# Seven products for eight in the first unweighted group of a fused attention and routed-MoE kernel

## The chip, the cores and the metric

The kernel runs on one core of a Trainium2 chip, in fp32 throughout. The metric is the device time of one execution in microseconds, as a median of several executions. The engines are named as the profile names them: PE is TensorE (matmuls; PEld are its weight loads), DVE is VectorE, ACT is ScalarE, POOL is GpSimd and SP is SyncE, which only issues DMAs. PSUM is the memory that TensorE writes to, here used as eight banks of 128 partitions x 512 fp32.

## The reference

Two stages, joined by `x`. The first is a linear attention with a polynomial sketch as feature map; the second routes all rows over eight experts with balanced weights and adds up eight two-layer networks.

```python
# q, k, v: (4, 4, 1088, 32); S1, S2: (8, 32)
phi(x): a = S1 x;  b = S2 x;  features = all products a_i * b_j      # 64 features
kv  = sum over s of phi(k) v;  z = sum over s of phi(k)
x   = (phi(q) kv) / (phi(q) z + 1e-6)                                # -> x: (4352, 128)

P = exp(x @ w_gate - max)                                            # (4352, 8)
for _ in range(8):
    P /= P.sum(1) + 1e-9;  P /= P.sum(0) + 1e-9;  P *= N / E
out = sum over e of P[:, e] * (relu(x @ w1[e]) @ w2[e])              # w1: 128x1024, w2: 1024x128
```

## The kernel before

**One stream of steps.** TensorE's work of the second stage is cut into steps by a generator. The work of attention and of the routing is put between these steps: `fill(n)` takes steps from the generator until their shares add up to n, and every `yield n` of `attention(b)` or `routing()` is passed to `fill`. So the experts' matmuls fill the time in which attention waits for other engines. What can be computed before the routing weights exist is done without them (the unweighted groups) and kept in `kept`; weights are multiplied in later.

```python
# (first column, columns of a tile, tiles, experts, weighted)
groups = [(0, 256, 2, [0], False), (512, 288, 2, [0], False), (0, 256, 2, [1], False),
          *((1088 + 832 * i, 416, 2, [0], False) for i in range(3)), (3584, 384, 2, [0], False),
          (512, 384, 2, [1], False)]
DIRECT = (0,)
# ... five weighted groups of three tiles and a last one of two follow
```

An item is a group with one of its experts; an item of a two-tile group has four blocks of two rows of 128 hidden units by two tiles of columns. A block has four steps; each step is one first-layer product, made of two matmuls in the two halves of the array (64 output rows each), and a ReLU on ScalarE:

```python
def first(k, f, lo, hi, out, flip):
    ph = bank()[:, 0:hi - lo]
    for s in (1, 0) if flip else (0, 1):
        nc.tensor.matmul(ph[64 * s:64 * s + 64], w1[...], x[:, lo:hi], ..., tile_position=(0, 64 * s))   # L926
    nc.scalar.activation(out=out, in_=ph, func=Act.Relu)                                                 # L930
```

**The second layer of a block.** Its products follow eight steps (`LAG`) behind its first layer. A plain block is a 2x2 by 2x2 product of matrices with eight half products (`eight`). The others take the known scheme with seven (`seven`), which needs sums of weights `ws` (four GpSimd additions per expert, made once), and per block differences of hidden units on VectorE (one operation of two tiles, two of one tile):

```python
def eight(k):            # only groups in DIRECT; two PSUM banks
    return [[(w2[:, 2 * q + c // 2, 64 * s:64 * s + 64], h[c], c % 2, s, 0) for s in range(2)] for c in range(4)]

def seven(k):            # all other two-tile groups; four PSUM banks s0 .. s3
    ...                  # p1 .. p7, from w2, ws, h and the differences ts
    return bank0, [p2, p4], bank2, [p7]     # p7 is alone in its step

def sums(c):             # inside two(k): VectorE, L943
    if direct_of(j):
        return
    ...
    elif c == 4:
        less(t13, later_h, earlier_h)           # two tiles at once
    elif c == 5:
        less(ts[2], h[3], ts[0])
        less(ts[3], h[2], ts[2])

share = n / 480 * (16 / 15 if g in DIRECT else 1)     # what a step yields to fill
```

When the sums of a direct group are complete, two ScalarE copies put them into `kept`. For the others `part_of_seven` makes nine ScalarE copies and six VectorE additions.

**Attention of the first batch element** ends with quotients: numerators and denominators are made by TensorE (`fractions`) and divided on VectorE (`divide`), in three chunks of columns.

```python
def bank():              # next of the four rotating PSUM banks, tag "a"
    ...
def fractions(c, m):
    t = queries[0, c, "pn", m] = mps.tile([P, 512], F32, tag=f"s{m + 2}", name="s") if c else bank()
    for i in range(2):
        nc.tensor.matmul(t[64 * i:64 * (i + 1), 0:n], kvz..., phs[0]..., ...)        # L404

def divide(c):           # VectorE: transpose pd (L415), add 1e-6, reciprocal,
    ...                  # transpose back (L420), multiply pn into xT (L422)
```

The order in which it is entered, with steps between:

```python
        query_products(2, 0); keys_products(1, 0)      # L387; VectorE L336
        fill(0.75)
        query_products(2, 1)
        multiply(2, 0)                                  # VectorE L396, reads a bank of query_products
        keys_products(1, 1)
        fill(0.75)
        multiply(2, 1)
        fill(0.75)
        fractions(2, 1); fractions(2, 0)
        keys_products(1, 2)
        fill(0.75)
        divide(2)
        ...
        fill(0.5)
        for b in range(1, B):
            for n in attention(b):
                fill(n)
```

**Attention of the other batch elements:**

```python
    def attention(b):
        keys_sums(b)                    # TensorE L352, one bank()
        times(b, 0)                     # VectorE L465: in place, features of a times b
        yield 2.2 if b == 1 else 2
        keys_kept(b)
        times(b, 1)
        tops(b, 0)                      # TensorE L474, L478
        if b == 1:
            transpose_q(2)              # VectorE L302
        yield 1.4
        times(b, 2)
        over(b, 0)                      # VectorE L487, L489, L493
        tops(b, 1)
        ...
        over(b, 2)
        take_over(b, 0, W9, nc.gpsimd)  # DMAs from GpSimd's queue, L498, L500
        yield 0.7
        keys_ab(b + 1)                  # TensorE L319, L324
        yield 0.7
        if b == 1:
            transpose_q(3)              # VectorE L302
        keys_products(b + 1, 0)
        yield 1.4
        keys_products(b + 1, 1)
        if b == 1:
            queries_ab(3)               # TensorE L438
        ...
```

`times(1, ...)` needs `rb`, which a DMA brings (`repeat_b`).

Of the kernel before, what the change touches and what calls it, by code (L numbers as in the profile page):

```python
# [10 lines left out]
F32 = mybir.dt.float32  # L11
# [39 lines left out]
def kernel(  # L51
# [13 lines left out]
    P = nc.NUM_PARTITIONS  # L65
# [20 lines left out]
    mps = ctx.enter_context(tc.tile_pool(name="mps", bufs=1, space=PSUM))  # L86
# [7 lines left out]
    def bank():  # L94
        return aps.tile([P, 512], F32, tag="a", name="a")
# [56 lines left out]
    for i in range(2):  # L152
        t = wk.tile([P, H + 1, NT + 1, D], F32, name=f"v{i}", bufs=1)
# [144 lines left out]
    keys, queries = {}, {}  # L298
# [42 lines left out]
    def keys_sums(b):  # L341

        kp, vx = products.pop(b), v_slots[b % 2]
        pv = bank()[:, 0:128].rearrange("p (i c d) -> p i c d", i=2, c=2)

        slots = [slice(h, H + 1, H - h) for h in range(H)]

        for t in range(NT + 1):
            n = P if t < NT else 64
            for h in range(H):  # L350
                i, s = divmod(h, 2)
                nc.tensor.matmul(pv[64 * s:64 * (s + 1), i], kp[0:n, H * t + h].rearrange("p i j -> p (i j)"),  # L352
                                 vx[0:n, slots[h], t, :], start=(t == 0 and i == 0), stop=(t == NT and i == 1),
                                 tile_position=(0, 64 * s))
        sums_of[b] = pv
# [42 lines left out]
    def fractions(c, m):  # L398

        lo, hi = chunks[c]  # L400
        n = hi - lo
        t = queries[0, c, "pn", m] = mps.tile([P, 512], F32, tag=f"s{m + 2}", name="s") if c else bank()
        for i in range(2):
            nc.tensor.matmul(t[64 * i:64 * (i + 1), 0:n], kvz[:, m, i].rearrange("p h d -> p (h d)"),  # L404
                             phs[0][:, i, lo:hi], start=True, stop=True, tile_position=(0, 64 * i))
# [57 lines left out]
    def times(b, c):  # L463
        ph = third(phs[b % 2], c)
        nc.vector.tensor_tensor(ph, ph, third(rb, c), op=Alu.mult)  # L465
# [53 lines left out]
    def attention(b):  # L519


        follows = b + 1 < B
        keys_sums(b)
        times(b, 0)
        yield 2.2 if b == 1 else 2
        keys_kept(b)
        times(b, 1)
        tops(b, 0)
        if b == 1:
            transpose_q(2)  # L530
        yield 1.4
        times(b, 2)
        over(b, 0)
        tops(b, 1)
        if b == 1:
            queries_ab(2)
            repeat_a(2)
        if follows:
            repeat_b(b + 1)
        yield 1.4  # L540
        over(b, 1)
        if b + 1 == B:
            take_over(b, 0, 192, nc.gpsimd)
        yield 1.4
        tops(b, 2)
        if follows:
            transpose_k(b + 1)
        if b + 2 < B:
            load_k(b + 2)
            load_v(b + 2)  # L550
        yield 1.4
        over(b, 2)
        if b + 1 < B:
            take_over(b, 0, W9, nc.gpsimd)
        else:
            take_over(b, 192, W9, nc.sync)
        if follows:
            yield 0.7
            keys_ab(b + 1)
            yield 0.7  # L560
            if b == 1:
                transpose_q(3)
# [4 lines that stand above are left out]
                queries_ab(3)  # L567
                repeat_a(3)
            yield 1.4
            keys_products(b + 1, 2)  # L570
            yield 1.4
# [75 lines left out]
    PLAIN = len(groups)  # L647


    DIRECT = (0,)  # L650
    for lo in (1280, 512, 2048, 2816, 3584):
        groups.append((lo, NT3, 3, list(range(2 if lo == 512 else 1, E)), True))
    groups.append((0, 256, 2, list(range(2, E)), True))
# [3 lines left out]
    items = [(g, e) for g, group in enumerate(groups) for e in group[3]]  # L657
    loaded_w, sources, sums, parts, done = {}, {}, {}, {}, {}
    soon, later = [], []

    def direct_of(j):
        return items[j][0] in DIRECT

# [3 lines left out]
    def prepare_w(j):  # L667
        g, e = items[j]
        three = groups[g][2] == 3
        if j == 0:  # L670
            loaded_w[j] = first_w
        elif items[j - 1][1] == e or not groups[g][4]:
            before = [i for i in range(j) if items[i][1] == e and i in loaded_w]
            loaded_w[j] = loaded_w[before[-1]] if before else load_w(e, False)
            if three and tiles_of(j - 1) == 2:
                loaded_w[j] = *loaded_w[j][0:2], sums_of_four(e, loaded_w[j][1])
        else:
            loaded_w[j] = load_w(e, not three, again=groups[g][4])
            if three:
                if g == len(groups) - 2 and e in groups[-1][3]:  # L680
                    sums_of_two(e, loaded_w[j][1], True)
                loaded_w[j] = *loaded_w[j][0:2], sums_of_four(e, loaded_w[j][1])
# [46 lines left out]
    def part(g, k):  # L729

        if g in DIRECT:
            lo, n, _, es, _ = groups[g]
# [359 lines left out]
    def into(g, w, x, i, s, place):  # L1092

        lo, n, t, es, _ = groups[g]
        if g not in sums:
            banks = range(2 * g, 2 * g + 2) if g in DIRECT else range(4)
            sums[g] = [mps.tile([P, 512], F32, tag=f"s{i % 4}", name="s")[:, 0:n * (t - 1)] for i in banks]
# [6 lines left out]
        per = len(es) * (FO // (4 if t == 3 else 2)) * TIMES[t][i][s]  # L1104
        if g in DIRECT:
            per = FO
# [14 lines left out]
    def steps():  # L1121

        todo, sums_at, t = {}, {}, 0
        for k in range(len(blocks) + 5):
            if k == len(blocks) - 2:
                ctx.enter_context(tc.manual_schedule(engines={engines.DVE, engines.PE, engines.Activation}))
            if k == len(blocks):
                for i, ps in enumerate(last_products()):
                    todo.setdefault(t + i, []).extend(ps)
            if k < len(blocks):  # L1130
                j, q = blocks[k]
                g, e = items[j]
                lo, n, tiles, es, weighted = groups[g]
                if q == 0:
                    for i in (j, j + 1, j + 2 if 0 < j and j + 2 < first_weighted else j):
                        if i < len(items) and i not in sources and (pools or i < first_weighted):
                            prepare_x(i)
                        if i < len(items) and i not in loaded_w and (pools or i < first_weighted):
                            prepare_w(i)
                if j == 0 and q == 2:  # L1140
                    prepare_w(2)
                if q == 1 and j + 1 < first_weighted and not direct_of(j + 1) and loaded_w[j + 1][2] is None:
                    w1, w2, _ = loaded_w[j + 1]
                    w = w1, w2, sums_of_two(items[j + 1][1], w2)
                    loaded_w.update({i: w for i in loaded_w if items[i][1] == items[j + 1][1]})
                if q == 0:
                    if weighted and 1 <= es.index(e) <= es[0] + 1:
                        weigh_kept(g, es.index(e) - 1)
                if k == len(blocks) - HELD:
                    kept_to_sums(g)  # L1150
                m, step, sums_ = (four if tiles == 3 else two)(k)
                products = twenty if tiles == 3 else eight if g in DIRECT else seven
            for c in range(m if k < len(blocks) else 4):
                if k < len(blocks):
                    step(c)
                for do in sums_at.pop(t, ()):
                    do()
                while soon:
                    soon.pop(0)()
                for b, p in todo.pop(t, ()):  # L1160
                    second(b, p)
                if k < len(blocks) and c == 0:
                    for i in range(2, 10):
                        sums_at.setdefault(t + i, []).append(lambda i=i, f=sums_: f(i))
                    if k < len(blocks) - 2:
                        for i, ps in enumerate(products(k)):
                            todo.setdefault(t + LAG + i, []).extend((k, p) for p in ps)
                share = n / 480 * (16 / 15 if g in DIRECT else 1)
                if k >= len(blocks):
                    while later:  # L1170
                        later.pop(0)()
                elif later and (tiles == 3 or c % 2 or share > 0.9):
                    later.pop(0)()
                yield share
                t += 1
        while soon:
            soon.pop(0)()
        while later:
            later.pop(0)()
# [105 lines left out]
```

## Time and profile before

| quantity | before |
|---|---|
| time, median of 3 | 920.73 us (920.6 to 921.01) |
| span of the profiled execution | 919.0 us |
| PE matmul records (two for each fp32 matmul) | 7450 |
| idle time that PE spent waiting for named engines | 3.0 us in five waits |
| DVE, ACT, POOL busy | 75%, 46%, 23% |

How to read it: the profile is of one execution. Its page gives busy time by engine, the chain of work that ended last, and groups of instructions; L with a number is the line of the kernel before. Groups such as `a<-xT,w` name output and inputs: `a` is a rotating PSUM bank, `s` one of the banks of sums, `hb` hidden units, `kp` products of keys, `ph` products of queries. Records of TensorE overlap, since the two halves of its array work side by side, and the ends of matmuls are modelled.

### The profile page before, as it was taken

The numbers are of one execution on the slowest core, as the hardware profiler recorded it, in microseconds if no ns is written. First come the engines' busy times: TensorE is split into PE (matmuls) and PEld (weight loads), VectorE is DVE, ScalarE is ACT, GpSimd is POOL, SyncE is SP. The second block draws the span as 40 slices with busy tenths as digits, with TensorE's granted clock in tenths as the row PEclk, the third lists the DMA queues.
The fourth block names the chain that finished last, engine by engine and source line by source line (L and its number), as shares of the span: only waits on it lengthen the run. The fifth ranks groups of instructions, "written<-read, shape, count | busy, mean of one in ns | idle before, by whom it ended". The sixth has DMA issues, their size and how long they took to land.

```text
span 919.0 us, 18917 instructions
## 1 busy us (share of the span) xinstructions
PE 911.0 (99%) x7450; PEld 602.8 (66%) x7450; DVE 689.6 (75%) x1173; ACT 421.9 (46%) x915; POOL 213.9 (23%) x220
## 2 busy tenths in 40 slices
PE   8999999999999999999999999999999999999997
PEld 6877544466666666666666666666666666667775
DVE  8678699888887798656985666956667976768664
ACT  3355465554444454444544444544445444446443
POOL 5021100175545422200210011110100343321120
PEclk9999999999999999999999999999999999999999
DMA  9995100213454545534364343463435556553650
GB/s 253 292 277 174 54 1 1 70 64 116 155 151 142 172 134 161 178 110 147 114 179 142 112 148 109 129 193 120 139 116 172 149 150 190 168 165 93 175 153 13
DMA packets 91305, 128.15 MB, mean 139 GB/s; under 512 B 25392, under 2 KB 69504, under 8 KB 86480
## 3 DMA queue, kind: packets, MB, share of 16 engines
q1 hardware_dynamic: 88384, 121.42, 43.3%
q0 software_dynamic: 1600, 5.36, 2.0%
q8 instruction: 58, 0.95, 0.4%
q10 hardware_dynamic: 1232, 0.16, 0.1%
q14 instruction: 31, 0.25, 0.1%
HBM read 107.88 MB, written 19.05 MB: 138 GB/s over the span
## 4 chain that ended last, share of the span: by engine, by line
PE 97%; DVE 1%; DMA 1%; issue 0%; ACT 0%; SPq 0%; DVEq 0%; ACTq 0%
PE a L926 52%; PE s L1111 42%; PE a L352 1%; PE a L474 1%; DMA kx<-in_k_dram 1%; PE a L319 0%; DVE hb L943 0%; PE s L381 0%; PE a L438 0%; PE s L404 0%; PE a L508 0%; PE a L387 0%; PE a L404 0%; DVE cs L614 0%; DVE rs L608 0%
## 5 line engine op out<-in xcount | busy, mean ns | idle before, releaser
L926 PE MATMUL a<-xe,w 128*64 128x256 f32 (+1 forms) x2560 | 562.5, 470 | 0.0
L930 ACT ACTIVATE hb<-a 128x256 f32<-128x256 f32 (+4 forms) x408 | 195.2, 481 | 242.4 <-PE a L926 211.8
L926 PEld LDWEIGHTS a<-xe,w 128*64 128x64 f32 x2560 | 247.1, 137 | 67.7 <-issue 1.9
L930 ACT ACTIVATE hx<-a 128x256 f32<-128x256 f32 (+1 forms) x360 | 167.3, 465 | 213.4 <-PE a L926 195.6
L1111 PE MATMUL s<-hb,ws 128*64 128x256 f32 (+3 forms) x1312 | 252.4, 395 | 0.2 <-DVE hb L943 0.2
L1111 PE MATMUL s<-hx,ws 128*64 128x256 f32 x1280 | 230.8, 379 | 0.0
L990 DVE TENSOR_TENSOR hb<-hb 128x512 f32<-128x512 f32 (+1 forms) x204 | 140.9, 700 | 96.0 <-ACT hb L930 91.9
L990 DVE TENSOR_TENSOR hx<-hx 128x512 f32<-128x512 f32 (+1 forms) x204 | 152.7, 759 | 61.2 <-ACT hx L930 55.6
L690 POOL TENSOR_TENSOR xe<-xT,xe 128x768 f32<-128x768 f32 (+2 forms) x41 | 83.4, 2034 | 481.9 <-DMA xe<-pT 383.1
L1111 PEld LDWEIGHTS s<-hb,ws 128*64 128x64 f32 x1312 | 127.2, 137 | 95.4 <-issue 67.4
L1111 PEld LDWEIGHTS s<-hx,ws 128*64 128x64 f32 x1280 | 125.1, 137 | 80.5 <-issue 53.8
L926 PE MATMUL a<-xT,w 128*64 128x416 f32 (+3 forms) x512 | 120.2, 462 | 0.0
L1111 PE MATMUL s<-hb,w 128*64 128x256 f32 (+3 forms) x536 | 113.7, 408 | 0.0
L1111 PE MATMUL s<-hx,w 128*64 128x256 f32 x384 | 75.1, 379 | 0.0
L943 DVE TENSOR_TENSOR hb<-hb 128x416 f32<-128x416 f32 (+7 forms) x84 | 60.3, 718 | 17.2 <-ACT hb L930 12.8
L1111 PEld LDWEIGHTS s<-hb,w 128*64 128x64 f32 x536 | 53.1, 137 | 20.1 <-issue 6.9
L926 PEld LDWEIGHTS a<-xT,w 128*64 128x64 f32 x512 | 50.1, 137 | 24.3 <-issue 15.3
L242 POOL TENSOR_TENSOR ws<-w 128x256 f32<-128x256 f32 (+1 forms) x70 | 61.7, 916 | 6.5 <-DMA w<-in_moe_w_dram 5.3
L943 DVE TENSOR_TENSOR hx<-hx 128x256 f32<-128x256 f32 (+1 forms) x65 | 39.4, 610 | 24.1 <-ACT hx L930 22.9
L1111 PEld LDWEIGHTS s<-hx,w 128*64 128x64 f32 x384 | 38.9, 137 | 8.4
L990 DVE TENSOR_TENSOR pqg<-hb 128x512 f32<-128x512 f32 x68 | 44.2, 691 | 0.0
L990 DVE TENSOR_TENSOR pqg<-hx 128x512 f32<-128x512 f32 x68 | 35.0, 554 | 0.0
(184 smaller groups left out, 489.1 us busy)
## 6 DMA issues: line engine op xcount, KB each, us to landing
w<-in_moe_w_dram SPq DMA_DIRECT2D x82, 512.0 KB, 5.5
ws<-ws SPq DMA_DIRECT2D x34, 1024.0 KB, 5.0
xe<-pT SPq DMA_DIRECT2D x34, 384.0 KB, 4.3
ws<-ws SPq DMA_DIRECT2D x12, 512.0 KB, 3.8
ph<-qa SPq DMA_DIRECT2D x12, 288.0 KB, 4.5
rb<-qb SPq DMA_DIRECT2D x3, 1152.0 KB, 8.0
pb<-pT SPq DMA_DIRECT2D x6, 384.0 KB, 7.5
kx<-in_k_dram SPq DMA_DIRECT2D x4, 544.0 KB, 4.7
```

The costliest lines, as they stand in the source:

```text
L242: tc.keep_in_program_order(nc.gpsimd.tensor_tensor(ws[:, c:c + len(ns)], blocks(x), blocks(y), op=Alu.subtract if off else Alu.add))
L352: nc.tensor.matmul(pv[64 * s:64 * (s + 1), i], kp[0:n, H * t + h].rearrange("p i j -> p (i j)"), vx[0:n, slots[h], t, :], start=(t == 0 an ...
L474: nc.tensor.matmul(pn[64 * s:64 * (s + 1), t, 2 * i:2 * i + 2].rearrange("p h d -> p (h d)"), ph[:, i, s, 64 * t:64 * (t + 1)], kvs[b % 2] ...
L690: tc.keep_in_program_order(nc.gpsimd.tensor_tensor(out, x, pb, op=Alu.mult))
L926: nc.tensor.matmul(ph[sl], loaded_w[j][0][:, P * f + H2 * s:P * f + H2 * (s + 1)], sources[j][:, lo:hi], start=True, stop=True, tile_posit ...
L930: nc.scalar.activation(out=out, in_=ph, func=Act.Relu)
L943: nc.vector.tensor_tensor(out, a, b, op=Alu.subtract)
L990: nc.vector.tensor_tensor(out if not isinstance(out, tuple) else places(*out), places(*a), places(*b) if isinstance(b, tuple) else b, op=A ...
L1111: nc.tensor.matmul(sums[g][i][H2 * s:H2 * (s + 1), n * place:n * (place + 1)], w, x, start=c == 1, stop=c == per, tile_position=(0, H2 * s))
```

## The change

Group 0 (columns 0 to 511, expert 0, columns in tiles of 256) is taken out of `DIRECT`: it too takes the scheme with seven products for eight. What goes with it:

- The weight sums of expert 0 are formed at the first step of the first item, on GpSimd.
- Group 0 now needs all four banks of sums s0 to s3. Two of them were used by the last chunk's quotients (`fractions(2, m)`), which now take two of the four rotating banks.
- A step of group 0 loses the factor 16/15 in its share.
- In `attention(1)`, `times(1, 0)` comes after 1.2 of the 2.2 that were filled behind it, so it stands later in VectorE's order.

It is for removing one of eight half products of the second layer in four blocks.

```diff
-        t = queries[0, c, "pn", m] = mps.tile([P, 512], F32, tag=f"s{m + 2}", name="s") if c else bank()
+        t = queries[0, c, "pn", m] = mps.tile([P, 512], F32, tag=f"s{m + 2}", name="s") if c == 1 else bank()
...
         keys_sums(b)
+        if b == 1:
+            yield 1.2
         times(b, 0)
-        yield 2.2 if b == 1 else 2
+        yield 1 if b == 1 else 2
...
-    DIRECT = (0,)
+    DIRECT = ()
...
+                if j == 0 and q == 0:
+                    w1, w2, _ = loaded_w[0]
+                    w = w1, w2, sums_of_two(0, w2)
+                    loaded_w.update({i: w for i in loaded_w if items[i][1] == 0})
```

## The prediction

> **What bounds the kernel now.** I first read the page's busy times and the summary of the chain that ended last, because a change that removes TensorE work is worth its full length only if TensorE is that chain.
>
> ```profile
> PE 911.0 (99%) x7450; PEld 602.8 (66%) x7450; DVE 689.6 (75%) x1173; ACT 421.9 (46%) x915; POOL 213.9 (23%) x220
> PE 97%; DVE 1%; DMA 1%; issue 0%; ACT 0%; SPq 0%; DVEq 0%; ACTq 0%
> ```
>
> It is: 911.0 of 919.0 us busy, 97% of the chain. So anything that keeps TensorE waiting costs its full length, and the other engines matter only where they make it wait. Next, TensorE's waits (columns: who waited, for whom, total us, times, longest us):
>
> ```profile
> PE a L319 <- DVE kT L307: 1.0, 1, 1.0
> PE a L404 <- ACT kvz L367: 0.6, 1, 0.6
> PE a L474 <- ACT hb L930: 0.2, 1, 0.2
> PE s L1111 <- DVE hb L943: 0.2, 1, 0.2
> ```
>
> With 1.0 us at the very start (L114, not shown) these are some 3 us in all. The changed group's 16 steps lie at about 16 to 48 us, so I tabulated that part (columns: stretch; its length; busy time with count of PE, PEld, DVE, ACT, POOL; clock; DMA share; GB/s):
>
> ```profile
> 22.20:28.70 6.50, 6.50 (x63) 6.50 (x61) 5.19 (x11) 3.27 (x10) 0.00 (x0) 1.00 0.84 236
> 28.70:34.90 6.20, 5.98 (x107) 4.41 (x103) 1.09 (x3) 2.09 (x7) 0.00 (x0) 1.00 0.94 350
> 34.90:58.00 23.10, 23.10 (x297) 18.49 (x299) 20.00 (x30) 9.53 (x25) 7.18 (x12) 1.00 1.02 307
> ```
>
> VectorE is already 80% busy in the first stretch and 87% in the third; only between 28.7 and 34.9 has it room. TensorE's timeline (start, duration, operation, records; each fp32 matmul leaves two records) then gives the places where attention's products meet the stream:
>
> ```profile
> 28.56 2.52 PE L352 MATMUL a<-v,kp 128*64 128x64 f32 x72
> 34.07 0.60 PE L1111 MATMUL s<-hb,w 128*64 128x256 f32 x4
> 34.89 0.92 PE L474 MATMUL a<-kvs,ph 128*64 128x66 f32 x24 [0.22 <-ACT hb L930]
> 51.97 0.54 PE L438 MATMUL a<-qT,wdq 128*64 128x192 f32 x2
> ```
>
> and VectorE's timeline gives what these need:
>
> ```profile
> 22.19 1.22 DVE L336 TENSOR_TENSOR kp<-ab 128x1024 f32<-128x1024 f32 x1
> 23.33 0.45 DVE L396 TENSOR_TENSOR ph<-ph,a 128x288 f32<-128x288 f32 x1
> 24.83 0.45 DVE L396 TENSOR_TENSOR ph<-ph,a 128x288 f32<-128x288 f32 x1
> 26.70 0.48 DVE L415 STREAM_TRANSPOSE rd<-s 128x288 f32<-128x288 f32 x1 [1.10 <-PE s L404]
> 33.83 1.83 DVE L465 TENSOR_TENSOR ph<-ph,rb 128x768 f32<-128x768 f32 x2 [5.11 <-DMA rb<-qb]
> 47.67 2.42 DVE L943 TENSOR_TENSOR hb<-hb 128x288 f32<-128x288 f32 x1
> 50.50 1.31 DVE L302 STREAM_TRANSPOSE qT<-qx 128x1088 f32<-128x1088 f32 x1
> ```
>
> The transpose of the next queries (L302) ends at 51.81 and its product L438 starts at 51.97: it is in time by 0.16 us.
>
> **What the Trainium skill says.** "TensorEngine Tiling (Array Packing)", Key Properties, says that different tiles of the array can execute in parallel. The trace agrees: four records (two half-array matmuls of 256 columns) start 0.43 us after the four before them, while one record alone is shown with some 0.38 us. So a removed half product is worth half of 0.43 us, provided that its neighbours can pair up.
> "VectorE: DVE Perf Modes", The TRN2 errata, gives an fp32 two-operand add as (N+151)/0.96 ns, 691 and 424 ns for N of 512 and 256; the trace has 666 and 419 ns as means of the unweighted stage's differences of these sizes.
> "SBUF — State Buffer", Who interferes with whom, says that a VectorE instruction with two SBUF inputs contends with a GpSimd instruction that reads SBUF. The line at 47.67 agrees: that 288-column difference took 2.42 us, others of its shape 0.46 us, and GpSimd formed sums of the next expert's weights from 47.67 to 49.76.
> "Perfetto Trace Analysis", Optimizing Tensor Performance, Matmuls, says that independent groups should rotate through PSUM banks. The change takes two of attention's tiles from the sums' banks and puts them into the rotation of four, so a bank's last reader now matters; the before trace cannot show that.
>
> **The change part by part.**
> 1. Removed from TensorE: group 0 has one expert and four blocks. Each had eight half products of the second layer and now has seven; 4 x 1 x 0.431/2 = 0.86 us less. Nothing else leaves TensorE; the first layer's matmuls stay, and so do attention's and those of all other groups.
> 2. The step loses its factor 16/15, so a step counts 0.533 and not 0.569; the 16 steps come about one step earlier against attention. TensorE's total is the same, but it is further on in time when it reaches an attention product.
> 3. That removes a wait. Before, the last matmul before L474 ends at about 34.50 (34.07 plus a pair's 0.43), and L474 starts at 34.89. The profile names ScalarE, which had long been done; the product with b (L465) started at 33.83, when its DMA landed, and one takes about 0.92 us, to 34.75, and that is what L474 needs. Later, TensorE reaches this point after 35, so 0.4 us disappear.
> 4. Added to VectorE: per block one 128x512 and two 128x256 differences. In the same form for another group they run from 63.35 to 64.95, 1.60 us together, about 1.4 us of pitch; 4 x 1.4 = 5.6 us. At the group's end six adds of 256 columns, about 0.37 us each, 2.2 us. ScalarE gets nine copies for two, below its 46% load. GpSimd's work is the same as before in the same order.
> 5. What these meet first, 22 to 30 us. I wrote VectorE's new order with the durations above: the block's difference comes before the product of keys of 22.19, and then the two small ones, so that the multiplications of 23.33 and 24.83 move to about 24.7 and 26.2. Each is the last reader of a bank of the rotation of four or the input of L404: TensorE waits about 0.3 us for a bank and 0.4 us for the second half of L404. The quotient then ends at about 30.3 for 28.7, and L352, the 72 records of 28.56, now takes a bank that this quotient has to free: about 0.5 us. Sum +1.2 us.
> 6. At 50 us: VectorE ran without a gap from 42.37 to its 0.65 us pause at 56.55. It now has the six adds in front, and GpSimd's weight sums (they wait for attention's transposes) move later with it and still block about 2 us. I get the end of L302 at 53.6 to 54.7, with TensorE at L438 at about 53.1: 0.5 to 1.6 us of new wait, and the least certain entry, since each us that TensorE loses in 5 shrinks it, and the 1.8 us pause of VectorE ahead of 42.37 may take in part of the adds.
> 7. Between 62 and 75 us, small waits, with an odd half product that finds no partner beside attention: 0.2 to 0.4 us.
> Behind the last product of keys of the attention part both kernels have the same work left, and routing and the weighted groups are untouched. So the difference there is final.
> Sum: -0.86 - 0.4 + 1.2 + 0.3 + (0.5 to 1.6) = +0.7 to +1.8 us on my walk. I take a third of it back: the order and the placement of one product were evidently chosen to avoid such waits, and a walk by hand adds up waits that in truth shorten each other. I predict +0.5 us, 921.2 us.
>
> **The rivals.**
> The gain arrives whole: 5 and 6 come to little, because VectorE catches up in the empty stretch after 28.7. For it: 1.09 us busy of 6.20 there. Against: L352, before that stretch, has no slack, and L302 sits behind an 87% busy stretch. It makes 919.5 to 919.9 us.
> VectorE becomes the bound from 22 to 58 us: all of 5, 6 and 7 in full. For it: 0.16 us of slack at L438; against: it idles 5.11 us at 28.7 to 33.8. It makes 922 to 923 us.
> The removed product was hidden anyway, since TensorE only waits longer at the next DMA, the landing of b at 33.83: then 920.7 us. Against: by the order, TensorE comes there after the landing.
>
> **Range and chances.** The range runs from nearly the whole gain to all of the new waits: 919.7 to 922.6 us. 2% are 18 us, some twenty times the removed work and ten times the largest wait I can name, so "within 2%" is all but certain: 0.01 faster, 0.98 same, 0.01 slower.
>
> **What would show it.** TensorE should have eight matmul records fewer, and its busy time should fall by less than 1 us. Step 3 is right if L474's wait near 35 is gone; step 5 if L404 and L352 show waits below 31 us and L352 starts at about 30.4; step 6 if L438 waits for L302 of VectorE and GpSimd's sums stand beside a long difference near 51 us. If L438 shows no wait, the time is about 920 and my walk was too pessimistic. If waits show in the weighted stage, my claim that all ends by 84 us is wrong.

## The result and the profile after

The change makes the kernel slower: 924.11 us (median of 6, 923.27 to 926.08) beside 920.7 us for the kernel before on the same chip; ratio 1.0040, 95% interval 1.0027 to 1.0053. That is 3.4 us more, above the predicted 921.2 and outside its range of 919.7 to 922.6 us. A later measurement (e12), on another chip, gave 925.0 us for 920.17.

The page of the changed kernel, busy times and the summary of the chain that ended last:

```profile
PE 913.8 (99%) x7442; PEld 599.6 (65%) x7442; DVE 693.2 (75%) x1191; ACT 423.7 (46%) x922; POOL 214.0 (23%) x220
PE 92%; DVE 4%; DMA 2%; ACT 1%; issue 1%; SPq 0%; DVEq 0%; ACTq 0%
```

TensorE has eight records fewer, as it should, and yet is busy 2.8 us longer. The chain now runs through VectorE for 4% of the span (1% before). TensorE's waits name the place (lines have moved by two: L928 is the old L926, L1113 the old L1111, L945 the old L943; L438, L352, L302 are where they were):

```profile
PE a L438 <- DVE qT L302: 2.1, 1, 2.1
PE s L1113 <- DVE hb L945: 0.6, 2, 0.4
PE a L352 <- DVE xT L422: 0.3, 1, 0.3
```

The wait of L404 (0.6 us) is as before and not shown. The first line is new: L438 makes the projections of the last batch's queries, and L302 is VectorE's transpose of these queries. TensorE's timeline at the places that the prediction looked at:

```profile
30.50 2.46 PE L352 MATMUL a<-v,kp 128*64 128x64 f32 x72 [0.31 <-DVE xT L422]
...
35.97 0.40 PE L474 MATMUL a<-kvs,ph 128*64 128x66 f32 x4
...
48.49 0.34 PE L319 MATMUL a<-wd,kT 128*64 128x64 f32 x3
...
52.95 0.83 PE L1113 MATMUL s<-hb,w 128*64 128x288 f32 x3
55.84 1.30 PE L438 MATMUL a<-qT,wdq 128*64 128x192 f32 x12 [2.06 <-DVE qT L302]
```

L438 starts 3.87 us later than before (55.84 for 51.97). VectorE's timeline ahead of it, and GpSimd's beside it:

```profile
42.95 1.10 DVE L945 TENSOR_TENSOR hb<-hb 128x576 f32<-128x576 f32 x1 [2.38 <-ACT hb L932]
...
51.46 2.55 DVE L752 TENSOR_TENSOR z<-z,w 128x256 f32<-128x256 f32 x1
54.05 0.42 DVE L752 TENSOR_TENSOR kept<-z,f 128x256 f32<-128x256 f32 x1
54.39 1.30 DVE L302 STREAM_TRANSPOSE qT<-qx 128x1088 f32<-128x1088 f32 x1
```

```profile
51.62 0.74 POOL L204 TENSOR_TENSOR ws<-ws,w 128x256 f32<-128x256 f32 x1
...
53.01 0.72 POOL L206 TENSOR_TENSOR ws<-w,ws 128x256 f32<-128x256 f32 x1
```

The transpose of these queries now stands behind five of the six additions that end group 0 (L752 and L755 are two of the helper's lines). One addition took 2.55 us where its neighbour took 0.42: it lies over GpSimd's three sums of expert 1's weights. Before, the same meeting hit a difference (2.42 us), but then the transpose still came in time.

One thing more is in the windows after the wait (stretch; length; busy of PE, PEld, DVE, ACT, POOL; granted clock; DMA share; GB/s):

```profile
56.00:57.00 1.00, 1.00 (x14) 0.98 (x14) 1.00 (x2) 0.00 (x0) 0.00 (x0) 0.90 0.98 407
57.00:58.00 1.00, 1.00 (x8) 0.63 (x6) 0.93 (x3) 0.00 (x0) 0.00 (x0) 0.50 1.02 422
58.00:59.00 1.00, 1.00 (x8) 0.63 (x6) 0.94 (x3) 0.41 (x1) 0.00 (x0) 0.50 1.02 395
59.00:60.00 1.00, 1.00 (x7) 0.63 (x6) 1.00 (x1) 0.00 (x0) 0.00 (x0) 0.50 1.13 239
60.00:61.00 1.00, 1.00 (x11) 0.79 (x9) 0.72 (x3) 0.41 (x1) 0.49 (x1) 0.89 0.98 173
```

For some 3.4 us TensorE's clock is at half: 0.10 + 3 x 0.50 + 0.11 = 1.7 us lost. That accounts for 1.7 us of a busy time that rises by 2.8 us while work is removed. It does not seem to happen in every execution: of eleven (six here, five of e12), the six with a mean clock of 0.998 took 924.96 to 926.08 us, the five with 0.999 or 1.000 took 923.27 to 924.21 us. Only two of the eleven are profiled, both among the six, and both show the half clock; for the others it is inferred from their times. The mean alone does not show it: it is 0.998 in e14's profiled execution, too, where the clock falls only behind TensorE's last product.

**The sum made again.** Up to the last batch's keys (L319) the changed kernel is about level. It starts them 0.97 us later (48.49 for 47.52), but by the order of instructions it then has, of each of the experts' two layers, two half products fewer left to do, some 0.9 us. From there to L438 both kernels do the same number of the experts' half products, give or take one. In the kernel before:

```profile
47.52 1.13 PE L319 MATMUL a<-wd,kT 128*64 128x64 f32 x32
...
51.96 0.41 PE L1111 MATMUL s<-hb,w 128*64 128x288 f32 x1
```

It takes 4.45 us for this, up to L438 at 51.97; the changed kernel takes 7.35 us, 2.9 us more. The list of waits has only 2.06 us, since it counts the time in which no product ran at all. Before, L438 started 0.01 us behind a product of the stream and ran beside it; behind the late transpose it could not. The 2.9 us agree with the difference in the executions at full clock (2.6 to 3.7 us), and 1.7 us come on top where the clock falls.

### The profile page after: what moved, and what is told of

Read it like the earlier page. It is cut to its first block, busy times and chain, and to the rows that moved or that the text cites. A ratio compares the mean times of both kernels' runs of the same rounds, so it can differ in the third digit from the quotient of the medians.

```text
span 924.0 us, 18934 instructions
## 1 busy us (share of the span) xinstructions
PE 913.8 (99%) x7442; PEld 599.6 (65%) x7442; DVE 693.2 (75%) x1191; ACT 423.7 (46%) x922; POOL 214.0 (23%) x220
## 4 chain that ended last, share of the span: by engine, by line
PE 92%; DVE 4%; DMA 2%; ACT 1%; issue 1%; SPq 0%; DVEq 0%; ACTq 0%
PE a L928 55%; PE s L1113 35%; DMA kx<-in_k_dram 1%; DVE hb L945 1%; PE a L352 1%; DMA v<-in_v_dram 1%; PE a L474 0%; DVE z L752 0%; DVE rd L489 0%; DVE kT L307 0%; DVE kp L336 0%; ACT hb L932 0%; PE a L438 0%; PE a L508 0%; DVE ph L465 0%
## 5 line engine op out<-in xcount | busy, mean ns | idle before, releaser
L928 PE MATMUL a<-xe,w 128*64 128x256 f32 (+1 forms) x2560 | 691.9, 470 | 0.0
L928 PEld LDWEIGHTS a<-xe,w 128*64 128x64 f32 x2560 | 320.4, 137 | 112.9 <-issue 1.6
L1113 PE MATMUL s<-hb,ws 128*64 128x256 f32 (+3 forms) x1344 | 340.9, 395 | 0.6 <-DVE hb L945 0.6
L1113 PE MATMUL s<-hx,ws 128*64 128x256 f32 x1280 | 306.2, 379 | 0.0
L1113 PEld LDWEIGHTS s<-hb,ws 128*64 128x64 f32 x1344 | 162.8, 137 | 72.5 <-issue 15.9
L1113 PEld LDWEIGHTS s<-hx,ws 128*64 128x64 f32 x1280 | 154.4, 137 | 57.4
L1113 PE MATMUL s<-hb,w 128*64 128x256 f32 (+3 forms) x496 | 131.5, 410 | 0.0
L928 PE MATMUL a<-xT,w 128*64 128x416 f32 (+3 forms) x512 | 124.4, 467 | 0.1
L1113 PE MATMUL s<-hx,w 128*64 128x256 f32 x384 | 95.6, 379 | 0.0
L945 DVE TENSOR_TENSOR hb<-hb 128x416 f32<-128x416 f32 (+7 forms) x96 | 65.0, 677 | 21.2 <-ACT hb L932 17.4
L1113 PEld LDWEIGHTS s<-hb,w 128*64 128x64 f32 x496 | 58.5, 137 | 20.8 <-issue 7.2
L928 PEld LDWEIGHTS a<-xT,w 128*64 128x64 f32 x512 | 52.2, 138 | 25.5 <-issue 17.5
L945 DVE TENSOR_TENSOR hx<-hx 128x256 f32<-128x256 f32 (+1 forms) x65 | 38.9, 603 | 24.5 <-ACT hx L932 23.4
L1113 PEld LDWEIGHTS s<-hx,w 128*64 128x64 f32 x384 | 46.2, 137 | 11.7 <-DVE hx L945 0.3
```

The costliest lines, as they stand in the source:

```text
L928: nc.tensor.matmul(ph[sl], loaded_w[j][0][:, P * f + H2 * s:P * f + H2 * (s + 1)], sources[j][:, lo:hi], start=True, stop=True, tile_posit ...
L945: nc.vector.tensor_tensor(out, a, b, op=Alu.subtract)
L1113: nc.tensor.matmul(sums[g][i][H2 * s:H2 * (s + 1), n * place:n * (place + 1)], w, x, start=c == 1, stop=c == per, tile_position=(0, H2 * s))
```

## The experiments

Each time stands beside that of the kernel before, measured together with it (920.49, 920.14, 920.28, 920.17, 920.17, 920.09 and 920.44 us in the order of the runs).

### What makes the transpose late: e3, e4, e7

e3 leaves out the six additions that end group 0:

```diff
 def part_of_seven(g, k):
+    if g == 0:
+        # two banks copied to kept, two to scratch, nothing combined
+        return
```

> The changed kernel, but group 0's four banks of sums are only copied out by four ScalarE copies; the six VectorE additions and five of nine copies that combine them are left out, so the columns 0 to 511 of expert 0 are not what the reference has. If the six additions, about 2.2 us, are what makes the transpose late, the wait of L438 falls from 2.06 to about 0 to 0.4 us and the time to 921 to 922 us. If the delay comes in earlier, from the blocks' differences at 22 to 31 us, the wait stays above 1.2 us and the time above 922.5 us.

e4 leaves out GpSimd's sums for expert 1:

```diff
 def sums_of_two(e, w2, again=False):
+    if e == 1 and not again:
+        return loaded_w[0][2]
```

> The changed kernel without GpSimd's four sums of expert 1's weights: its groups use those of expert 0, so these groups' values are not the reference's; the count of matmuls stays. If GpSimd's reads stretch the VectorE addition at 51.5 us from 0.42 to 2.55 us, that addition takes about 0.42 us here, the transpose ends 2.1 us earlier and the wait of L438 is 0 to 0.2 us, the time 921 to 922 us. If the long duration has another cause, the addition stays near 2.5 us and the time near 924 us.

e7 computes everything, but forms these sums two blocks later:

```diff
-                if q == 1 and j + 1 < first_weighted and not direct_of(j + 1) and loaded_w[j + 1][2] is None:
+                if q == (3 if j == 1 else 1) and j + 1 < first_weighted and not direct_of(j + 1) and ...
```

> The changed kernel with GpSimd's four sums of expert 1's weights entered two blocks later, so that they stand behind attention's DMAs of batch 1 on GpSimd and run at about 62.7 to 65.6 us, where VectorE idled from 63.4 to 66.8 us; they are used from about 71 us on. If it is the meeting of these sums with VectorE's additions that makes the transpose late, the addition takes 0.42 us, the wait of L438 falls under 0.3 us, as in the run without the sums, and the time is 920.9 to 921.7 us. If not, 924 us.

Measured: e3 921.27 us (ratio 1.0008, 1.0000 to 1.0017), e4 921.32 us (1.0009, 1.0001 to 1.0017), e7 921.28 us (1.0011, 1.0004 to 1.0017). None of the three has a wait at L438 in the list. VectorE's timeline in e7:

```profile
50.78 0.42 DVE L752 TENSOR_TENSOR z<-z,w 128x256 f32<-128x256 f32 x1
...
51.57 1.30 DVE L302 STREAM_TRANSPOSE qT<-qx 128x1088 f32<-128x1088 f32 x1
```

The addition is back at 0.42 us and the transpose ends at 52.87 instead of 55.69. e4 and e7 take away the meeting with GpSimd and leave the additions, and no wait is recorded: so the additions alone do not make it. e3 takes away more than the additions. Without them GpSimd's sums fall beside the transpose itself (still 1.30 us) and the product of keys behind it (L336, 2.13 us; 1.18 us in e7), so nothing ahead of the transpose is stretched and it ends at 50.62 us. What the meeting does without the additions is therefore not shown. Each of the three runs is 2.3 to 4 us below the changed kernel (which is 3.4 and 4.8 us above the kernel before in its two measurements).

The list of waits hides a part: in e4 and e7 L438 starts 0.15 us behind the end of the transpose, exactly as in the changed kernel, where TensorE does wait (55.69 to 55.84). So there the transpose still sets when L438 starts, while other products run; only in e3 is it early, by 1.65 us. Some 1 us against the kernel before stays in all three, although 0.86 us of TensorE's work is gone by step 1.

### Moving the transpose: e1, e2

```diff
         if follows:
             repeat_b(b + 1)
+        if b == 1:
+            transpose_q(3)
         yield 1.4
...
-            if b == 1:
-                transpose_q(3)
             keys_products(b + 1, 0)
```

> The changed kernel with one VectorE instruction elsewhere: the transpose of the last queries (L302) is entered after the second of the middle batch's three tiles of query products, where VectorE idled 2.4 us, instead of behind the group's additions. If the new time is the wait of TensorE for this transpose (2.06 us, and the lower clock that follows it in some executions), the wait is gone, the clock is 1.000 in all executions, and the time falls from about 924 to 921.0 to 921.7 us. If the quotients' banks or VectorE's load as a whole are the cause, the wait only moves to the next product that needs VectorE and the time stays within 0.7 us of 924.

> The kernel before with the same move of the transpose. Before, the transpose was in time (by 0.16 us), so both theories expect 920.7 us, within 0.3 us; a fall of more would mean that the move brings something else than the removed wait, and the reading of the first run must be corrected by it.

Both missed what was expected. e1 took 923.13 us (1.0032, 1.0020 to 1.0043) and e2, the same move in the kernel before, 923.48 us (1.0035, 1.0023 to 1.0048). The wait at L438 is gone, but the place that looked idle was not free: the queries are loaded only then. VectorE in e1:

```profile
42.98 1.31 DVE L302 STREAM_TRANSPOSE qT<-qx 128x1088 f32<-128x1088 f32 x1 [2.85 <-DMA qx<-in_q_dram]
```

All that is entered behind this instruction on VectorE ran behind it and waited for the load with it: 2.85 us in e1, 4.96 us in e2. In e1 the keys (L319) then wait 0.48 us for VectorE. This pair says nothing for or against the cause; it exchanged one wait of VectorE's for another.

### The small parts of the change: e5, e6

e5 is the kernel before with the new banks and the later product only; e6 is the changed kernel without the later product:

```diff
# e5, against the kernel before
-        t = ... if c else bank()
+        t = ... if c == 1 else bank()
...
         keys_sums(b)
+        if b == 1:
+            yield 1.2
         times(b, 0)
-        yield 2.2 if b == 1 else 2
+        yield 1 if b == 1 else 2
```

```diff
# e6, against the changed kernel
         keys_sums(b)
-        if b == 1:
-            yield 1.2
         times(b, 0)
-        yield 1 if b == 1 else 2
+        yield 2.2 if b == 1 else 2
```

> The kernel before with the two smaller parts of the change alone: the last chunk's quotients in the rotating banks and the batch 1 product with b later; group 0 keeps its eight products. If the bank change costs by itself, keys_sums (L352) waits for the quotient's last VectorE operation: in the trace of before that operation ends at 28.7 and L352 starts at 28.56, so the wait is at most 0.2 us, and the later product may cost up to 0.4 us at L474: 920.5 to 921.1 us. If the rotating banks are the main cause of the loss, 922 us or more.

> The changed kernel with batch 1's first product with b where it was before. VectorE then stands at this product until its DMA lands (about 33 us) and forms block 2's differences after it instead of at 30.6 to 32.2 us. TensorE uses them from about 33.4 us on, so I expect a new wait of about 1.5 us at a product with ws near 33.5 us and 1.3 to 2 us more than the changed kernel, 925 to 926 us. If the later place of the product is without use, 924 us as the changed kernel.

e5: 919.96 us (0.9999, 0.9991 to 1.0008). The new banks and the later product together cost the kernel before nothing that these runs can show. e6: 924.72 us (1.0053, 1.0040 to 1.0067), so the later product is worth little; the wait of 1.5 us near 33.5 us that I expected is not there, a bank is waited for 0.44 us at 41.1 us instead, and L438 waits 1.85 us. After that wait the clock stayed whole in the profiled execution:

```profile
56.00:57.00 1.00, 0.86 (x11) 0.89 (x13) 1.00 (x1) 0.00 (x0) 0.00 (x0) 1.00 0.98 393
```

### What the removed products are worth: e14, e15, e17, e10, e18

These take the kernel before and leave out four half products of group 0 with nothing in their place (one tile's values are then incomplete), so they have the gain of the change without its price. e14 leaves out one per block, always in the second half of the array; e15 one per block, the halves in turn, as the change does; e17 two whole pairs, in the third and fourth block:

```diff
-    return [[(w2[...], h[c], c % 2, s, 0) for s in range(2)] for c in range(4)]
+    return [[(w2[...], h[c], c % 2, s, 0) for s in range(2 if c < 3 else 1)] for c in range(4)]      # e14
+    return [[(...) for s in range(2) if c < 3 or s == k % 2] for c in range(4)]                      # e15
+    return [[(...) for s in range(2) if c < 3 or k < 2] for c in range(4)]                           # e17
```

> The kernel before with one of eight half products per block of group 0 left out and nothing put in its place, so half of one tile's values of that group is incomplete: what the removed product is worth by itself, without VectorE's differences, additions and new banks. By my sum 0.86 us, less what is lost at the product with b at 34.9 us, whose DMA does not land earlier (up to 0.4 us): 919.3 to 919.9 us where before takes 920.2. If a single half product beside a missing partner takes as long as a pair, nothing is gained: 920.0 to 920.4 us.

> The kernel before with one of eight half products left out in each of group 0's four blocks, in turn from the second and the first half of the array, in the step where the change has its single product; nothing is put in its place, so one tile's values are incomplete. The run that left out four, all of one half, gained nothing, which it could not: the other half's row of products stayed as long. If the two halves make up for each other from block to block, 0.86 us are gained here, less up to 0.4 at the product with b: 919.3 to 919.9 us beside 920.2. If attention's products between the blocks bring the halves together again, so that each single product takes the place of a pair, the time is 920.0 to 920.4 us.

> As the run before, but the four half products left out are two pairs, both halves of one step in the third and the fourth block; these lie behind the product with b at 34.9 us. A pair out takes its 0.43 us from both halves, so both readings expect 0.86 us less, 919.2 to 919.6 us beside 920.2. If this too gains nothing, the time is set by what attention waits for and not by the count of products, and both readings fall.

Measured: e14 920.31 us (1.0000, 0.9992 to 1.0008), e15 920.56 us (1.0003, 0.9995 to 1.0011), e17 920.21 us (1.0002, 0.9994 to 1.0010). None gains. The traces show what each saved behind the product with b: from L474 near 35 us to the first second-layer product behind L319 (48.99 us in the kernel before) it takes 14.10 us before, 14.10 in e14, 13.78 in e15 and 13.23 in e17. So e14 saved nothing; the other half's row of products was as long as before, and my expectation of it was badly thought out. e15 has three of its single products in this stretch and saved 0.3 us, half of the 0.65 us that step 1 charges for three. e17's two pairs saved 0.87 us, and yet its time is that of the kernel before. The trace shows where the 0.87 us went. In e17:

```profile
46.63 1.13 PE L319 MATMUL a<-wd,kT 128*64 128x64 f32 x32
...
51.08 0.65 PE L1112 MATMUL s<-hb,w 128*64 128x288 f32 x2
51.93 1.20 PE L438 MATMUL a<-qT,wdq 128*64 128x192 f32 x12 [0.21 <-DVE qT L302]
```

At L319 e17 is 0.9 us ahead (46.63 for 47.52); L438 starts at 51.93 where the kernel before started it at 51.97. The recorded wait is only 0.21 us, because a last product of the stream ran on until 51.73. In both kernels the transpose ends at 51.8:

```profile
50.48 1.30 DVE L302 STREAM_TRANSPOSE qT<-qx 128x1088 f32<-128x1088 f32 x1
```

L438 starts 0.15 us behind that end in e17, 0.16 in the kernel before, and 0.15 in the changed kernel. So the 0.16 us were no reserve: in the kernel before VectorE already sets when L438 can start, and what TensorE saves ahead of it is lost there. If this is so, the saving must come out once the transpose is early. e10 is the kernel before with the late sums of e7, e18 is e17 with them.

> The kernel before with GpSimd's sums of expert 1's weights two blocks later, as a comparison for the same edit in the changed kernel. Before, these sums stretched one difference of VectorE to 2.42 us at 47.7 us, but the transpose still ended 0.16 us ahead of L438. Both theories expect no change beyond 0.3 us (919.9 to 920.5 us); a gain of more than 0.5 us would mean that the sums cost the kernel before something too.

> The kernel before with the two pairs of half products left out, and GpSimd's sums of expert 1 two blocks later. In the run with the pairs alone, TensorE was 0.8 us ahead at the keys (L319, 46.6 us for 47.5) and had lost all of it at L438 (51.93 for 51.97), which waited for the transpose that ends at 51.8 in both. If that is where the removed work went, here the transpose ends about 2 us earlier, TensorE keeps its 0.8 us, and the time is 919.2 to 919.6 us beside 920.1 (ratio 0.9990 to 0.9995). If a later meeting point (the product with b of batch 2, or the routing) sets the end as well, the time stays at 919.9 to 920.3 us.

e10 took 920.3 us (0.9999, 0.9991 to 1.0007): an earlier transpose alone gives nothing, for there TensorE is the later of the two (L438 is 2.15 us behind the transpose and, as before, 4.45 us behind L319). e18 took 919.54 us beside 920.44 (0.9990, 0.9983 to 0.9997): 0.9 us less (0.3 to 1.6 us by the interval), which fits the removed products' 0.86 us. VectorE and TensorE in e18:

```profile
47.67 1.30 DVE L302 STREAM_TRANSPOSE qT<-qx 128x1088 f32<-128x1088 f32 x1
```

```profile
50.52 0.54 PE L438 MATMUL a<-qT,wdq 128*64 128x192 f32 x2
```

The transpose is 1.5 us ahead of its use. Each of the two edits is worth nothing alone, both together are worth about the full length of the products. This is shown for pairs; what single products in turn (e15) would gain with the late sums was not run.

### Versions without the recorded wait: e8, e9, e11, e13, e16

All compute the whole and start from the changed kernel. e8 has the late sums, and moves VectorE's three differences of group 0's second block behind the last quotient, with the two multiplications of that chunk together. e9 is e8 with one step more ahead of TensorE's first use of batch 1's product with b (L474); e11 is e9 with the sums in their old place; e13 and e16 are e11 with that step given back at the routing, and behind batch 1.

```diff
-            elif c == 4:
+            elif c == (8 if k == 1 else 4):                # e8: and the two small ones with it
...
         multiply(2, 0)
+        multiply(2, 1)
         keys_products(1, 1)
         fill(0.75)
-        multiply(2, 1)
...
-        yield 1 if b == 1 else 2
+        yield 1.6 if b == 1 else 2                          # e9, e11, e13, e16
...
-        yield 5
+        yield 4.4                                           # e13, ahead of the logits
...
             keys_products(b + 1, 2)
-            yield 1.4
+            yield 0.8 if b == 1 else 1.4                    # e16
```

> The run before this one, and in addition VectorE's three differences of group 0's second block come after the last chunk's quotient instead of ahead of it (they are used only after L352), and the two multiplications of that chunk stand together. If the rest of the loss, about 0.8 us, lies in the waits at L404 and L352 between 26 and 31 us, both vanish here, L352 starts about 0.6 us earlier against the work done, and the time falls to 919.9 to 920.7 us. If the rest lies elsewhere (half products without a partner, waits after 60 us), the time stays at that of the run before, 920.9 to 921.7 us.

> The run with late sums and late differences, and one step of the experts more between keys_sums and the first product with b of batch 1 (1.6 shares for 1). In a slower execution of that run TensorE stood 0.6 us before L474 for the product with b, whose DMA had landed late, and 0.9 us for a bank that VectorE freed late after it. If its small loss against the kernel before (0.6 to 0.8 us) comes from arriving too early at what the DMA brings, one more step takes these waits away and the time is 919.7 to 920.4 us, at or below the kernel before. If it lies in half products without a partner and waits after 60 us, the time stays at 920.6 to 921.2 us.

> The changed kernel with the late differences of group 0's second block, the two multiplications together and one step more before batch 1's first product, but GpSimd's sums of expert 1 in their old place. In the run before with one step more, the late sums stood behind a DMA's landing and cost 1.3 us at 68 us in the profiled execution. Here they run right after the transposes of batch 1, at about 52.5 to 54.7 us, beside the transpose of the queries (one input) and a product of keys that TensorE needs only at 59 us. If the order of VectorE's work was what the change lacked, no wait over 0.5 us is left after 20 us and the time is 919.4 to 920.2 us. If the meeting of sums and additions still delays the transpose, L438 waits and the time is over 921 us.

> The run with late differences and one step more, and the step given back at the routing (4.4 shares for 5 ahead of the logits). Of the run without this, 11 of 21 executions took 919.6 to 920.7 us and nine 922.4 to 923.6 us; in the profiled one of the longer kind TensorE waited three times 0.5 us between 262 and 325 us for GpSimd's weighting of a group's columns. If these waits come from the routing weights arriving one step late against the work left, no execution is above 921 us here and the median is 919.6 to 920.2 us, 0 to 0.6 us under the kernel before. If they come from the way in which GpSimd's and VectorE's instructions happen to meet in the weighted group, the two kinds of executions stay.

> The run with late differences and one step more, with the step given back behind batch 1 (0.8 shares for 1.4), so that all after 60 us stands as in the changed kernel. Those executions that took 922.4 to 923.6 us there had waits for GpSimd in the weighted group. If they come from the shift of one step, they are gone and the time is 919.6 to 920.4 us; if not, some executions over 922 us stay.

| run | median us | ratio, 95% interval | what TensorE waits for in the profiled execution, beside the start |
|---|---|---|---|
| e8 | 920.78 | 1.0009, 1.0003 to 1.0016 | product with b 0.6, a bank 0.9, keys 1.1 |
| e9 | 920.60 | 1.0008, 0.9998 to 1.0018 | the late sums 1.3, keys 1.0 |
| e11 | 920.67 | 1.0013, 1.0004 to 1.0022 | weighting by GpSimd 3 x 0.5, a bank 0.3, keys 0.3 |
| e13 | 921.70 | 1.0016, 1.0010 to 1.0023 | logits for the DMA of x 0.4, a bank 0.3 |
| e16 | 921.23 | 1.0012, 1.0005 to 1.0018 | a bank 0.3 |

The profiled executions of e8 and e11 are among their longer ones (922.1 and 922.6 us). All five, like the changed kernel, also wait 0.4 to 0.5 us for a VectorE difference. The wait for the keys, near 7 us, differs between kernels that have the same work there (1.0 us in the kernel before, none in the changed one). e8 is 0.5 us under e7, but the intervals overlap, so what the waits of 26 to 31 us cost is not shown. None of the five reached the time that its expectation names for the theory it tests, and no version beats the kernel before; e9's interval alone takes in equality. e11 had the shortest executions beside e9: 11 of its 21 executions took 919.6 to 920.7 us, but eight (not nine, as the expectation of e13 has it) took 922.4 to 923.6 and one 925.3, with TensorE, in the profiled one of these, waiting for GpSimd in the weighted stage (first at 262 us, 0.50 us).

e13 and e16, which give the step back, have no execution over 922.3 us, so the long executions come with the shift of one step; both lose what e11's shorter executions had. e12 was the changed kernel once more:

> The changed kernel once more, on the chip of the experiments and beside the run before it. By the waits it should take 923.3 to 924.2 us with L438 waiting about 2 us for the transpose; where the clock stays full right after that wait, the time is 2 us under that of the executions where it falls.

It took 925.0 us (1.0050, 1.0037 to 1.0064), above the 923.3 to 924.2 us named, with a wait of 2.08 us at L438; four of its five executions had the lower mean clock (924.96 to 925.54 us), the fifth took 923.82 us.

## Why the prediction was wrong

**What held.** The eight records fewer; step 3 (L474 at 35.97 without a wait); step 4 (a block's three differences 1.61 us, an addition 0.42 us); step 5 nearly to the number (the multiplications at 24.84 and 26.34 for "about 24.7 and 26.2", L352 at 30.50 for 30.4, its wait 0.31 for 0.5). Steps 1, 3 and 5 together come to -0.06 us in the walk, and the changed kernel was about level at L319. Step 7's small waits came a little later than 62 to 75 us (0.15 us at 75.8 us, 0.11 at 83.2). That nothing follows behind 84 us was nearly right: one wait for a difference grew from 0.18 to 0.45 us at 167 us.

**Step 6 failed by its size.** Its mechanism and its place were right: L438 waits for L302, behind the additions and beside GpSimd's sums. I had the transpose end at 53.6 to 54.7 us, TensorE at L438 at about 53.1, and so 0.5 to 1.6 us. TensorE's last products ahead of L438 start from 52.95 us on, much as I had it, but the transpose ended at 55.69, so that L438 came 2.9 us late, of which the list has 2.06. The transpose is 3.88 us later than before. About 2.1 us of this are the five additions ahead of it, one of them stretched by GpSimd in place of a difference, much as step 6 says. The rest is what it overlooked. VectorE's pause ahead of 42.37, on which I counted to take in part of the additions, now ends at 42.95. And the quotients of batch 1's second tile (L487, L489, L493, 1.35 us together), which ran ahead of the pause, now stand behind it; the kernel before, then the changed one:

```profile
39.15 0.19 DVE L487 RECIPROCAL rc<-a 128x12 f32<-128x12 f32 x1
...
42.37 1.78 DVE L943 TENSOR_TENSOR hb<-hb 128x576 f32<-128x576 f32 x3 [1.81 <-ACT hb L930]
```

```profile
43.97 0.22 DVE L487 RECIPROCAL rc<-a 128x12 f32<-128x12 f32 x1
```

TensorE had finished their input by 40.0 us, but they are entered behind the difference of 42.95, which waits for ScalarE. So VectorE idled 2.38 us (1.81 before) with work at hand. This is read from the two traces; no run moves these quotients.

**Step 1 is no gain of its own.** I entered the products' 0.86 us in the sum as a gain. The sum still hangs together, because the wait of step 6 is counted from TensorE's arrival: the end of L302 at 53.6 to 54.7, less 51.97, less 0.9 us of work already done, gives the same +0.7 to +1.8 us. But it means that with this wait the end of the transpose alone sets the time, and all terms ahead of it drop out. e17 shows the same for the kernel before, where I read 0.16 us of reserve and there was none. The rival "hidden anyway" was the true one for the product there, at another place than the landing of b where I looked for it.

**The third taken back was wrong.** I argued that a walk by hand adds up waits that shorten each other. At L438 there was nothing to shorten: VectorE's end alone sets it. A third off +0.7 to +1.8 us would also have left +0.5 to +1.2, of which I named the lower end. The walk's upper end of +1.8 us was nearer than the +0.5 I named.

**Not foreseen at all** was the half clock after the wait, 1.7 us in the two profiled executions and, by their times, in about half of all. Without it the time is still above my range (923.27 to 924.21 us).

**What stays open:** the last 0.3 to 1.5 us by which the median of every full version without the recorded wait is above the kernel before. Small waits at several places show in these traces (a bank, the sums, the product with b, GpSimd's weighting), other ones in each version. In e8, e9, e11, e13 and e16 L438 also starts only 0.15 to 0.21 us behind the end of the transpose; in e11, e13 and e16 that is 5.40 us behind L319, where the kernel before takes 4.45 us for the same number of half products, and only 0.26 us of it is in the list (a bank). No run isolates any of this.

## What to carry to other kernels

Before counting removed work as a gain, find the next point where its engine meets another, and how early the other is there. Measure this reserve against a place where the engine does wait: 0.16 us from the end of the transpose to its use looked like a reserve, but where TensorE waited for it the distance was 0.15. A recorded wait can also be smaller than its cost (2.06 us for 2.9), since the list counts only the time in which the engine does nothing. Price added work on a side engine by the last thing behind it that the main engine waits for, not by its busy share (75% of VectorE here, before and after). And look for idle room by asking what the moved instruction itself needs: a gap on the engine is no gap if its data lands at the end of it.

## What the runs showed of the hardware

A wait of 2.06 to 2.08 us of TensorE was followed, in the two profiled executions that have one, by some 3.4 us at half clock (1.7 us lost); after one of 1.85 us (e6) the clock stayed at 1.00. The Trainium skill, "TensorE: Matmul & The Clock Gate", section "HAM oscillation — how this bites in real kernels", gives as a rule to have no gaps above about 3.4 us; here the clock fell behind the shorter gap, twice in the profiles and, by times and mean clock, in six of eleven executions. That the gap is the cause rests on the order in time; at which length it begins no run shows.

The same skill, "SBUF — State Buffer", Who interferes with whom, says that a VectorE instruction with two SBUF inputs contends with GpSimd's reads. The addition at 51.46 agrees: 2.55 us beside three GpSimd sums that last 2.1 us together, 0.42 us without them (e7).
